# The sign of float64 weights carried by the slope of a parametric ReLU

## The chip, the cores and the metric

The kernel runs on one core of one Trainium2 chip. A core has five engines that run side by side and wait for each other through semaphores: TensorE (PE) for matrix products, VectorE (DVE) and ScalarE (ACT) for element-wise work, GpSimd (POOL) for more element-wise work, and SyncE (SP), which here only issues DMAs. The metric is the time of one execution on the device, in microseconds (us).

## The reference

Chunked attention over 4 x 8 heads of 576 tokens, and then two MLPs on the 2304 tokens, of 512 to 2048 to 512 channels. Cut to what matters:

```python
scores = scale * np.matmul(q_c, k_c.transpose(0, 1, 2, 4, 3))     # chunks of 64 tokens
attn = np.exp(scores - np.max(scores, axis=-1, keepdims=True))
attn = attn / (np.sum(attn, axis=-1, keepdims=True) + 1e-09)
x = np.matmul(attn, v_c)                                          # then tokens x 512

h = x @ w_in                                                      # first MLP
x = (h * (1.0 / (1.0 + np.exp(-1.702 * h)))) @ w_out
h = x @ w_in2                                                     # second MLP: mish
out = (h * np.tanh(np.log1p(np.exp(h)))) @ w_out2
```

q, k and v are float32. The four weight matrices are float64, 8 MB each, since they are drawn as `np.random.randn(...) * c` without a cast.

## The kernel before

**Weights.** No engine computes in float64, so the kernel takes the weights as pairs of 32-bit words and builds float32 from them. Each MLP's weights are 32 pieces of 128 x 512 values (512 KB of float64), which alternate between `w_in` and `w_out`. A piece passes four stages, the methods of class `Weights`:
- `load` (L118, L123): a DMA issued by SP brings the words into a tile `raw`, the low and the high word of each value side by side.
- `scale` (L149): ACT multiplies the high word, read as a float32, by 2^-112. That takes 896 off the eleven-bit exponent. The line is `nc.scalar.mul`, which becomes one ACTIVATE.
- `join` (L159, L160, L163): three DVE instructions. L159 (a TENSOR_SCALAR) shifts the low word right by 29. L160 (a SCALAR_TENSOR_TENSOR) takes the sign bit out of the scaled high word and puts it into the low word. L163 (a SCALAR_TENSOR_TENSOR) shifts the high word left by 3, which pushes its own sign bit out, and puts the low word into it. The result is the float32.
- `split` (L184, L185): the products run as float32r in two parts, so ACT writes the rounded part (L184, a CAST), and POOL writes the rest (L185, a subtraction of two tensors).

For the second MLP the float32 goes back to DRAM between `join` and `split`.

**Stages in time.** Tokens run in 6 blocks of 384. The start, to about 130 us, holds the attention of the first block, the conversion of all 32 pieces of the first MLP, the first MLP's products on block 0 (16 steps of 128 hidden channels), and the attention of block 1. Then the first MLP runs over the other blocks while the pieces of the second are scaled and joined one every two steps. The second MLP fills the rest.

**Order.** Instructions are issued to each engine in the order in which they are written, with no scheduler. The first part of the start is written out in the string `PLAN`, one letter for each call (`c` scale, `j` join, `s` split, `l` load). After it comes a loop over steps; `convert()` is called twice in each of the first 16 steps, and each call splits one piece, joins the next and scales the one after. A step of the first block holds, on PE, 12 products for the in-projection (L337 to L339, tile `h`) and 12 for the out-projection (tile `acc`); on ACT a gelu (L355) and a cast (L359); on POOL the subtraction for the low part of the activations (`g_lo`, L364). Every five steps hold the attention of one tile of 128 tokens: transposes (L246), scores (L262), `shift` (L276, L277), exp (L282), sums, `normalize` on POOL (L293), transposes again, the products with v (L313), and `x_hi`, `x_lo` (L329, L333). ACT's exp and gelu need different tables, so an ACT_TABLE_LOAD stands between them.

Of the kernel before, what the change touches and what calls it, by code (L numbers as in the profile page):

```python
# [11 lines left out]
AF = mybir.ActivationFunctionType  # L12
ALU = mybir.AluOpType
AX = mybir.AxisListType
I32 = mybir.dt.int32
SIGN = -(2**31)

P = 128
CH = 64
TB = 384  # L20
# [4 lines left out]
LAG_B = 5  # L25
GROUP = 4
NRAW = 5
# The start, step by step, where attention, the first products and the weights' conversion share
# the engines: a letter (see `steps`) and the tile, the slot or how often.
PLAN = """  # L30
    w8 d0 d1 w8 T0 T1 w1 Q1 k0 K1 d2 q0 S0 M0 l S1 X0 T2 l v2 M1 N0 K2 l Q2 X1 S2 U0 c N1 c
    M2 j w17 l v0 A0 X2 N2 V0 c c j j v1 l U1 U2 A1 V1 P0 A2 d3 P1 s H0 V2 c w2 H1 s L0 P2 s
# [11 lines left out]
def tile_kernel(  # L44
# [8 lines left out]
    w_out2: bass.AP,  # L53
    out: bass.AP,
):
    """Chunked attention and two MLPs on one stream of tokens, in blocks of TB tokens.

    The products of the MLPs split each float32 operand exactly into two float32r parts and
    carry hi*hi, hi*lo and lo*hi. The first MLP runs over all blocks, with the attention of
    the next block between its products; then its weights give way to the second MLP's.  # L60
    """
    nc = tc.nc
    B, H, S, D = q.shape
    NT, DM = out.shape
# [7 lines left out]
    scale = 1.0 / math.sqrt(D)  # L72
# [9 lines left out]
    ident = const.tile([P, P], F32, name="ident")  # L82
    one = const.tile([P, 1], F32, name="one")

    # ---------------------------------------------------------------- weights
    class Weights:
        """The weights of one MLP, piece by piece: float64 words to float32r hi and lo.

        A float64's high word, read as a float32, has the upper eight bits of the exponent as
        its exponent; 2^-112 there takes 896 off the eleven-bit exponent, so that the word  # L90
        shifted up by three, with its sign and the top of the low word, is the float32.
        """

        def __init__(self, w_in, w_out, staged):
            self.w_in, self.w_out = w_in, w_out
# [31 lines left out]
            self.raw[i] = r  # L127

        def room(self, name):
            """Room for words: at first where the last half of the weights goes later."""  # L130
            if len(self.spare) > self.np // 2:
                return wres.tile([P, DM, 2], I32, tag=self.spare.pop(), name=name)
            return wraw.tile([P, DM, 2], I32, tag="raw", name=name)

        def load_ahead(self):
            """Loads for which there is room by now."""
            used = self.at["join" if self.staged is not None else "split"]
            while self.at["load"] < self.np and (
                len(self.spare) > KF or self.at["load"] - max(used, self.first) < self.ahead
            ):  # L140
                self.load()
                if len(self.spare) > KF:
                    self.first = self.at["load"]

        def scale(self):
            if (i := self._next("scale")) is None:
                return
            hi = self.raw[i][:, :, 1].bitcast(F32)
            nc.scalar.mul(hi, hi, 2.0**-112)  # L149

        def join(self):
            if (i := self._next("join")) is None:
                return
            r = self.raw.pop(i)
            lo, hi = r[:, :, 0], r[:, :, 1]
            to = hi
            if self.staged is not None:
                to = half_slot(f"wf{i}").bitcast(I32)
            nc.vector.tensor_scalar(lo, lo, 29, None, op0=ALU.logical_shift_right)  # L159
            nc.vector.scalar_tensor_tensor(  # L160
                lo, hi, SIGN, lo, op0=ALU.bitwise_and, op1=ALU.bitwise_or
            )
            nc.vector.scalar_tensor_tensor(  # L163
                to, hi, 3, lo, op0=ALU.logical_shift_left, op1=ALU.bitwise_or
            )
            if self.staged is not None:
                nc.sync.dma_start(out=self.staged[i], in_=to.bitcast(F32))
            else:
                self.f32[i] = to.bitcast(F32)
# [7 lines left out]
        def split(self):  # L177
            if (i := self._next("split")) is None:
                return
            key = kind, f = self.order[i]  # L180
            w = self.f32.pop(i)
            both = wres.tile([P, 2, DM], F32R, tag=f"w{kind}{f}", name=f"w{kind}{f}")
            hi, lo = both[:, 0], both[:, 1]
            nc.scalar.copy(hi, w)  # L184
            nc.gpsimd.tensor_tensor(out=lo, in0=w, in1=hi.bitcast(F32), op=ALU.subtract)  # L185
            self.hi[key], self.lo[key] = hi, lo

        def convert(self):
            """One step of the pieces on their way: each stage takes the next piece."""
            if self.at["join"] > self.at["split"] and self.staged is None:  # L190
                self.split()
            if self.at["scale"] > self.at["join"]:
                self.join()
            if self.at["load"] > self.at["scale"]:
                self.scale()
            if self.staged is not None or self.at["load"] > 4:
                self.load_ahead()

    def half_slot(name, t=None):
        t = wraw.tile([P, DM, 2], I32, tag="raw", name=name) if t is None else t  # L200
        return t.rearrange("p f w -> p (f w)")[:, 0:DM].bitcast(F32)

    # ---------------------------------------------------------------- attention
    xh, xl = {}, {}

    def load_tok(pool, tag, src, i):
        """128 tokens of all heads, token by partition."""
        t = pool.tile([P, H * D], F32, tag=tag, name=f"{tag}{i}")
        load_into(t, src, i)
        return t  # L210

    def load_into(t, src, i):
        done = 0
        while done < P:
            b, s = divmod(i * P + done, S)
            n = min(P - done, S - s)
            nc.sync.dma_start(
                out=t[done : done + n].rearrange("p (h d) -> p h d", h=H),
                in_=src[b, :, s : s + n, :].rearrange("h p d -> p h d"),
            )  # L220
            done += n

    class Attention:
        """The attention of 128 tokens, two chunks, for all heads: x^T in two parts."""

        def __init__(self, i, slots):
            self.i, self.slots = i, slots
# [53 lines left out]
        def exp(self):  # L281
            nc.scalar.activation(self.eg, self.eg, AF.Exp, scale=scale)  # L282
# [49 lines left out]
            hi, lo = self.xo  # L332
            nc.vector.tensor_tensor(out=lo, in0=self.x, in1=hi.bitcast(F32), op=ALU.subtract)  # L333

    # ---------------------------------------------------------------- products
    def mm3(o, wh, wl, mh, ml, start, stop):
        nc.tensor.matmul(o, wh, mh, start=start, stop=False)  # L337
        nc.tensor.matmul(o, wh, ml, start=False, stop=False)  # L338
        nc.tensor.matmul(o, wl, mh, start=False, stop=stop)  # L339
# [116 lines left out]
            r0 = j * TB + t * P  # L456
            nc.sync.dma_start(out=out[r0 : r0 + P, :], in_=o)

    # ---------------------------------------------------------------- program
    W = [Weights(w_in1, w_out1, False), Weights(w_in2, w_out2, True)]  # L460
    order_b = list(kept) + list(range(NB - 2))
    NA = NB * KF
# [6 lines left out]
    with tc.manual_schedule():  # L469
        at = at_cm.__enter__()  # L470
        every = ["at", "acc0", "acc1"]
        usual = ["at"]
        first = [Attention(i, every) for i in range(TT)]
# [5 lines left out]
        zeros = const.tile([P, TB], BF16, name="zeros")  # L479
# [3 lines left out]
        idle = ps.tile([P, TB], F32, tag="h", name="idle")  # L483
# [12 lines left out]
            load_into(tiles[i].v, v, i)  # L496

        def keep_warm(n):
            """Products of zeros while the data is on its way: an idle array halves its clock."""
            for _ in range(n):  # L500
                nc.tensor.matmul(idle, zeros[:, 0:P], zeros, start=True, stop=True)

# [3 lines left out]
        def split():  # L506
# [5 lines left out]
        steps = {  # L512
            "w": keep_warm,
            "d": load_tile,
            "v": load_v,
            "l": lambda _: w1.load(),
            "c": lambda _: w1.scale(),
            "j": lambda _: w1.join(),
            "s": lambda _: split(),
            "T": lambda i: tiles[i].transposes(),  # L520
# [31 lines left out]
        ends = set(range(NA + FIRST - 1, N - LAST, GROUP)) | {N - LAST - 1, N - 1}  # L552

        def lag(n):
            """How far the out-projection is behind: more from the last block of the first MLP on."""
            if n < NA - KF + LAG_A:
                return LAG_A
            return LAG_T if n < NA + LAG_T else LAG_B


        for n in range(4, N + LAG_B):
            f = n % KF
            # in-projection and activation
            if n < NA:
                j = n // KF
                hp[n] = in_proj(W[0], (xh[j], xl[j]), f)
# [5 lines left out]
            elif n < N:  # L572
# [6 lines left out]
                if n in ends:  # L579
# [5 lines left out]
                    for m in group:  # L585
                        mish_out(m)
                    group.clear()
            # the attention of the next block
            if n < NA - KF and f > 0:
                at_step = (f - 1) % 5  # L590
                if at_step == 0:
# [15 lines left out]
                elif at_step == 4:  # L607
# [1 line left out]
                    att.x_hi(act)  # L609
                    att.x_lo()  # L610
                    att = nxt
            # out-projection
            m = n - lag(n)
            if 0 <= m < NA and m == done:
                done += 1
# [3 lines left out]
            elif m >= NA:  # L619
# [4 lines left out]
                    out_b([m - 1, m], jb)  # L624
                if m % KF == KF - 1:
                    evac_b(jb)
            # weights that run ahead
            if n < KF:
                W[0].convert()
                if n == KF - 1:  # L630
# [10 lines left out]
            else:  # L641
                for _ in range(2):
# [4 lines left out]
                        break  # L647
                    W[1].split()
                    W[1].fetch()
            # room for the second MLP  # L650
            if n == NA - KF:
                at_cm.__exit__(None, None, None)
                tb = ctx.enter_context(tc.tile_pool(name="tb", bufs=5))
# [34 lines left out]
```

## Time and profile before

| | |
|---|---|
| median of 3 runs | 923.54 us (923.38 to 923.80) |
| the profiled execution: span from first to last instruction | 920.4 us |
| the median above that span | 3.1 us |
| PE busy | 884.2 us, 96% |
| DVE busy | 586.0 us, 64% |
| ACT busy | 435.2 us, 47% |
| POOL busy | 225.3 us, 24% |

No time of the profiled execution beyond its span is given, so the 3.1 us between its span and the median are taken as what lies around it.

The shares are means over a program whose stages differ: of the 40 slices of the page, 23 us each, DVE is at 90% or more in the second to the fifth, and below 80% in all others. In the chain of waits, each piece is the work that released the next one. A row of a timeline gives the start, the duration, the engine, the line, and in brackets the idle time just before and what ended it. Matmuls overlap each other, so their pitch (from start to start) is shorter than their duration.

### The profile page before, as it was taken

The numbers are of one execution on the slowest core, as the hardware profiler recorded it, in microseconds if no ns is written. First come the engines' busy times: TensorE is split into PE (matmuls) and PEld (weight loads), VectorE is DVE, ScalarE is ACT, GpSimd is POOL, SyncE is SP. The second block draws the span as 40 slices with busy tenths as digits, with TensorE's granted clock in tenths as the row PEclk, the third lists the DMA queues.
The fourth block names the chain that finished last, engine by engine and source line by source line (L and its number), as shares of the span: only waits on it lengthen the run. The fifth ranks groups of instructions, "written<-read, shape, count | busy, mean of one in ns | idle before, by whom it ended". The sixth has DMA issues, their size and how long they took to land.

```text
span 920.4 us, 14445 instructions
## 1 busy us (share of the span) xinstructions
PE 884.2 (96%) x5724; PEld 823.3 (89%) x5724; DVE 586.0 (64%) x986; ACT 435.2 (47%) x710; POOL 225.3 (24%) x188
## 2 busy tenths in 40 slices
PE   7768889999999999999999999999999999999997
PEld 5767779999999999999999989898989898989896
DVE  6999955456455655646532676676666766766765
ACT  5566644334333333433334654644645545546453
POOL 2565650000000000000156432231221322312312
PEclk9979899999999999999999999999999999999999
DMA  9926642445444633642344101001001001000000
GB/s 244 271 72 183 178 130 101 107 107 178 129 104 131 178 114 94 194 116 70 115 128 124 35 1 69 36 0 69 35 1 69 35 1 70 35 1 0 35 1 35
DMA packets 91940, 82.73 MB, mean 90 GB/s; under 512 B 58848, under 2 KB 75232, under 8 KB 91872
## 3 DMA queue, kind: packets, MB, share of 16 engines
q1 hardware_dynamic: 91872, 81.80, 30.8%
q8 instruction: 45, 0.74, 0.3%
q14 instruction: 23, 0.19, 0.1%
HBM read 62.39 MB, written 19.40 MB: 89 GB/s over the span
## 4 chain that ended last, share of the span: by engine, by line
PE 81%; DVE 12%; ACT 3%; issue 3%; DMA 1%; SPq 0%; POOLq 0%; DVEq 0%; ACTq 0%
PE h L337 13%; PE h L339 13%; PE h L338 13%; PE acc L337 7%; PE acc L338 6%; PE acc L339 6%; PE accb L447 4%; PE accb L446 4%; PE accb L445 4%; DVE raw L160 3%; DVE raw L163 3%; PE third L446 2%; PE third L447 2%; PE third L445 2%; DVE raw L159 2%
## 5 line engine op out<-in xcount | busy, mean ns | idle before, releaser
L337 PE MATMUL h<-xh,wi 128*128 128x384 f32 x512 | 173.9, 340 | 6.7 <-ACT t L355 5.2
L426 POOL TENSOR_TENSOR gl<-e,gh 128x384 fp32r<-128x384 f32 x96 | 108.4, 1129 | 288.0 <-DVE gh L425 286.6
L339 PE MATMUL h<-xh,wi 128*128 128x384 f32 x512 | 173.5, 339 | 1.0 <-POOL wi L185 1.0
L338 PE MATMUL h<-xl,wi 128*128 128x384 f32 x512 | 172.9, 338 | 0.7 <-DVE xl L333 0.7
L337 PE MATMUL acc<-gh,wo 128*128 128x384 f32 x384 | 135.5, 353 | 0.0
L359 DVE CAST gh<-t 128x384 fp32r<-128x384 f32 x80 | 34.5, 431 | 157.8 <-ACT t L355 156.6
L417 ACT ACTIVATE e<-e,one 128x384 f32<-128x384 f32 x96 | 59.2, 617 | 159.3 <-DVE e L412 159.2
L338 PE MATMUL acc<-gl,wo 128*128 128x384 f32 x384 | 129.7, 338 | 0.0
L339 PE MATMUL acc<-gh,wo 128*128 128x384 f32 x384 | 129.5, 337 | 0.0
L355 ACT ACTIVATE t<-h 128x384 f32<-128x384 f32 x96 | 47.1, 490 | 172.1 <-PE h L339 83.6
L337 PEld LDWEIGHTS h<-xh,wi 128*128 128x128 f32 x512 | 97.3, 190 | 9.9 <-ACT t L355 5.8
L338 PEld LDWEIGHTS h<-xl,wi 128*128 128x128 f32 x512 | 97.2, 190 | 1.9 <-DVE xl L333 1.1
L185 POOL TENSOR_TENSOR wi<-ws,wi 128x512 fp32r<-128x512 f32 x16 | 21.1, 1319 | 316.9 <-ACT wi L184 316.9
L339 PEld LDWEIGHTS h<-xh,wi 128*128 128x128 f32 x512 | 97.2, 190 | 1.4 <-POOL wi L185 1.3
L418 DVE TENSOR_TENSOR e<-e,hs 128x384 f32<-128x384 f32 x96 | 54.2, 564 | 64.1 <-ACT e L417 64.1
L337 PE MATMUL h<-x2h,wi 128*128 128x384 f32 x256 | 86.3, 337 | 0.0
L339 PE MATMUL h<-x2h,wi 128*128 128x384 f32 x256 | 86.2, 337 | 0.0
L338 PE MATMUL h<-x2l,wi 128*128 128x384 f32 x256 | 85.9, 336 | 0.0
L425 DVE CAST gh<-e 128x384 fp32r<-128x384 f32 x96 | 79.6, 829 | 9.4 <-DVE e L424 0.5
L447 PE MATMUL accb<-wo,gl 128*128 128x512 f32 x192 | 76.4, 398 | 1.0 <-POOL gl L426 1.0
L446 PE MATMUL accb<-wo,gh 128*128 128x512 f32 x192 | 75.8, 395 | 0.0
L337 PEld LDWEIGHTS acc<-gh,wo 128*128 128x128 f32 x384 | 73.1, 190 | 2.0
(97 smaller groups left out, 1668.5 us busy)
## 6 DMA issues: line engine op xcount, KB each, us to landing
raw<-in_moe_w_in_dram SPq DMA_DIRECT2D x32, 512.0 KB, 4.0
raw<-in_moe_w_out_dram SPq DMA_DIRECT2D x32, 512.0 KB, 3.8
w_f<-wf SPq DMA_DIRECT2D x32, 256.0 KB, 2.2
ws<-w_f SPq DMA_DIRECT2D x32, 256.0 KB, 2.7
out_dram<-o SPq DMA_DIRECT2D x18, 256.0 KB, 2.1
v<-in_v_dram SPq DMA_DIRECT2D x16, 256.0 KB, 5.7
q<-in_q_dram SPq DMA_DIRECT2D x13, 256.0 KB, 4.7
k<-in_k_dram SPq DMA_DIRECT2D x13, 256.0 KB, 5.3
```

Of the source, the lines that this page charges most:

```text
L337: nc.tensor.matmul(o, wh, mh, start=start, stop=False)
L338: nc.tensor.matmul(o, wh, ml, start=False, stop=False)
L339: nc.tensor.matmul(o, wl, mh, start=False, stop=stop)
L355: nc.scalar.activation(gt[n], hp.pop(n), AF.Gelu_apprx_sigmoid)
L359: (nc.scalar.copy if n < KF else nc.vector.tensor_copy)(gh[n], gt[n])
L417: nc.scalar.activation(e, e, AF.Ln, bias=one, scale=0.5)
L418: nc.vector.tensor_add(e, e, hs[n])
L425: nc.vector.tensor_copy(out=a, in_=z)
L426: nc.gpsimd.tensor_tensor(out=b, in0=z, in1=a.bitcast(F32), op=ALU.subtract)
L445: nc.tensor.matmul(o, a[:, ts], wh, start=f == 0, stop=False)
L446: nc.tensor.matmul(o, a[:, ts], wl, start=False, stop=False)
L447: nc.tensor.matmul(o, b[:, ts], wh, start=False, stop=f == KF - 1)
```

## The change

The scaling step becomes a parametric ReLU with scale 2^-112 and slope 2^32. A positive word is scaled as before. A negative word is scaled by 2^-112 and then by 2^32, which adds 32 to its eight-bit exponent; that sets bit 28 of the word, and the shift left by 3 in `join` moves bit 28 to bit 31, the sign of the float32. So L160 is no longer issued, 32 times for each MLP, 64 in all. Comments and docstrings are dropped as well; lines behind `join` have numbers lower by three in the changed kernel, where L160 is the step that is L163 before.

```diff
-SIGN = -(2**31)
...
             hi = self.raw[i][:, :, 1].bitcast(F32)
-            nc.scalar.mul(hi, hi, 2.0**-112)
+            nc.scalar.activation(hi, hi, AF.Prelu, scale=2.0**-112, alpha=2.0**32)
...
             nc.vector.tensor_scalar(lo, lo, 29, None, op0=ALU.logical_shift_right)
             nc.vector.scalar_tensor_tensor(
-                lo, hi, SIGN, lo, op0=ALU.bitwise_and, op1=ALU.bitwise_or
-            )
-            nc.vector.scalar_tensor_tensor(
                 to, hi, 3, lo, op0=ALU.logical_shift_left, op1=ALU.bitwise_or
             )
```

On DVE, in the loop of the first 16 steps, before the change (the number behind a tile's name counts tiles; three pieces and the `x_lo` of one attention tile):

```order
L159 TENSOR_SCALAR raw_588<-raw_588 128x512
L160 SCALAR_TENSOR_TENSOR raw_588<-raw_588 128x512
L163 SCALAR_TENSOR_TENSOR raw_588<-raw_588 128x512
L333 TENSOR_TENSOR xl_723<-pv_705,xh_722 128x2x4x64
L159 TENSOR_SCALAR raw_599<-raw_599 128x512
L160 SCALAR_TENSOR_TENSOR raw_599<-raw_599 128x512
L163 SCALAR_TENSOR_TENSOR raw_599<-raw_599 128x512
L159 TENSOR_SCALAR raw_641<-raw_641 128x512
L160 SCALAR_TENSOR_TENSOR raw_641<-raw_641 128x512
L163 SCALAR_TENSOR_TENSOR raw_641<-raw_641 128x512
```

The same place after it:

```order
L159 TENSOR_SCALAR raw_578<-raw_578 128x512
L160 SCALAR_TENSOR_TENSOR raw_578<-raw_578 128x512
L330 TENSOR_TENSOR xl_708<-pv_690,xh_707 128x2x4x64
L159 TENSOR_SCALAR raw_588<-raw_588 128x512
L160 SCALAR_TENSOR_TENSOR raw_588<-raw_588 128x512
L159 TENSOR_SCALAR raw_628<-raw_628 128x512
L160 SCALAR_TENSOR_TENSOR raw_628<-raw_628 128x512
```

One of three instructions of each piece is gone; nothing else on DVE stands in another place. On ACT, around the first exp among the gelus, before the change:

```order
L149 ACTIVATE raw_363<-raw_363 128x512
L282 ACT_TABLE_LOAD
L282 ACTIVATE e_502<-e_502 128x512
L184 CAST wo_581<-raw_359 128x512
L184 CAST wi_585<-raw_361 128x512
L355 ACT_TABLE_LOAD
L355 ACTIVATE t_593<-h_539 128x384
L149 ACTIVATE raw_365<-raw_365 128x512
```

And after it:

```order
L149 ACTIVATE raw_360<-raw_360 128x512
L279 ACT_TABLE_LOAD
L279 ACTIVATE e_496<-e_496 128x512
L181 CAST wo_571<-raw_356 128x512
L181 CAST wi_575<-raw_358 128x512
L352 ACT_TABLE_LOAD
L352 ACTIVATE t_582<-h_531 128x384
L149 ACTIVATE raw_362<-raw_362 128x512
```

No table load is added, there or anywhere else on ACT, and none moves. The orders of PE, POOL and SP are the same before and after.

## Rows read from the trace of the kernel before

**Rows 1.** The page: busy tenths of DVE in 40 slices of 23 us.
```profile
DVE  6999955456455655646532676676666766766765
```
**Rows 2.** Stretches: busy us (count) of PE, PEld, DVE, ACT, POOL; clock; DMA share, GB/s.
```profile
16.00:128.00 112.00, 84.74 (x655) 77.86 (x653) 105.78 (x120) 69.27 (x116) 68.26 (x50) 0.90 0.64 180
62.33:97.51 35.18, 26.89 (x200) 24.97 (x199) 33.13 (x37) 21.88 (x37) 22.94 (x16) 0.95 0.59 169
140.00:300.00 160.00, 160.00 (x1287) 155.42 (x1286) 89.43 (x169) 60.88 (x94) 0.00 (x0) 1.00 0.46 125
50.00:55.00 5.00, 2.06 (x8) 2.06 (x9) 4.79 (x7) 3.01 (x4) 2.77 (x2) 0.50 0.00 0
```
**Rows 3.** The chain of waits in order of time: start us, us, what.
```profile
59.27 1.62 DVE raw L160
...
130.28 0.69 PE pv L313 x32
...
144.54 1.08 PE sc L262 x32
...
168.80 1.08 PE sc L262 x32
```
**Rows 4.** Groups by line, DVE, 16 to 128 us: busy us, mean ns, idle before.
```profile
L163 DVE SCALAR_TENSOR_TENSOR raw<-raw 128x512 int32<-128x512 int32 x32 | 45.4, 1419 | 1.1
L160 DVE SCALAR_TENSOR_TENSOR raw<-raw 128x512 int32<-128x512 int32 x32 | 33.2, 1038 | 3.2 <-ACT wo L184 0.5
L159 DVE TENSOR_SCALAR raw<-raw 128x512 int32<-128x512 int32 x32 | 18.7, 586 | 0.0
```
**Rows 5.** Timeline of DVE: start us, us, engine, line, operation.
```profile
62.21 0.42 DVE L159 TENSOR_SCALAR raw<-raw 128x512 int32<-128x512 int32 x1
62.73 0.69 DVE L160 SCALAR_TENSOR_TENSOR raw<-raw 128x512 int32<-128x512 int32 x1
63.46 1.69 DVE L163 SCALAR_TENSOR_TENSOR raw<-raw 128x512 int32<-128x512 int32 x1
65.07 0.41 DVE L159 TENSOR_SCALAR raw<-raw 128x512 int32<-128x512 int32 x1
...
97.40 0.42 DVE L159 TENSOR_SCALAR raw<-raw 128x512 int32<-128x512 int32 x1
```
**Rows 6.** Timeline of POOL, two places.
```profile
63.06 1.54 POOL L185 TENSOR_TENSOR wo<-raw,wo 128x512 fp32r<-128x512 f32 x1 [1.33 <-ACT wo L184]
...
91.31 1.06 POOL L364 TENSOR_TENSOR gl<-t,gh 128x384 fp32r<-128x384 f32 x1 [1.50 <-ACT gh L359]
92.33 1.75 POOL L185 TENSOR_TENSOR wo<-raw,wo 128x512 fp32r<-128x512 f32 x1
```
**Rows 7.** Timeline of SP, PE and ACT: loads, and what uses them.
```profile
20.17 0.37 SPq L217 DMA_DIRECT2D k<-in_k_dram  x1
...
27.08 1.11 PE L246 MATMUL tr<-ident,q 128*128 128x128 f32 x4
...
87.01 0.37 SPq L118 DMA_DIRECT2D raw<-in_moe_w_in_dram  x1
...
93.52 0.70 ACT L149 ACTIVATE raw<-raw 128x512 f32<-128x512 f32 x1
```
**Rows 8.** The page: DMA issues, KB each, median us to landing.
```profile
raw<-in_moe_w_in_dram SPq DMA_DIRECT2D x32, 512.0 KB, 4.0
...
k<-in_k_dram SPq DMA_DIRECT2D x13, 256.0 KB, 5.3
```
**Rows 9.** Groups by line, ACT, whole run.
```profile
L149 ACT ACTIVATE raw<-raw 128x512 f32<-128x512 f32 x64 | 43.0, 675 | 0.0
L282 ACT ACT_TABLE_LOAD x15 | 19.2, 1283 | 0.2
L282 ACT ACTIVATE e<-e 128x512 f32<-128x512 f32 x17 | 10.8, 633 | 15.7 <-DVE e L277 15.7
```
**Rows 10.** Groups by line, DVE, 142 to 466 us.
```profile
L160 DVE SCALAR_TENSOR_TENSOR raw<-raw 128x512 int32<-128x512 int32 x32 | 22.2, 694 | 1.2
```

## Prediction

> **What bounds the kernel now.** I read the page first. DVE's row of busy tenths [rows 1] has two parts: 9 in the second to the fifth slice, 23 to 115 us, and 3 to 7 in all behind. So I cut the run near there. In the stretches [rows 2] DVE is busy for 105.8 of the 112.0 us from 16 to 128, PE for only 84.7 and ACT for 69.3; from 140 to 300 it is PE that has no idle time at all, 160.00 of 160.00. The start is DVE's, the rest is PE's. The chain of waits, read third, says the same in order of time: up to 128 us it consists of DVE's joins, such as L160 at 59.27, and from 130.28 on of PE [rows 3].
>
> The groups by line [rows 4] then tell what DVE does there: of its 105.8 us, 97.3 are the three instructions of the 32 joins (45.4 + 33.2 + 18.7). A piece in the loop starts at 62.21 and the next at 65.07, 2.86 us later [rows 5]. The stretch repeats itself every five steps, ten pieces and one attention tile: from 62.21 to 97.40, 35.19 us [rows 5]. PE does five such steps in 24.26 us where nothing holds it up (scores to scores, 144.54 to 168.80 [rows 3]), and ACT is busy for 21.9 us of such a cycle [rows 2]. So in the start DVE has 11 us a cycle to lose before PE is next.
>
> **What is removed.** L160, 64 times. The first 32 lie in the DVE stretch. Alone it takes 0.69 us, and the next instruction starts 0.73 us behind its start (62.73 to 63.46 [rows 5]). Its mean is 1038 ns though, and L163's 1419 [rows 4], with 1.69 in the row at 63.46 [rows 5]. The extra microsecond is POOL's: its subtraction L185 starts at 63.06, while L160 runs [rows 6], and L163 behind it is stretched by 1.00 us. Two POOL instructions back to back start 1.02 us apart (91.31 and 92.33 [rows 6]), so that is how long one holds DVE up. The Trainium skill has this as a rule (SBUF — State Buffer, section "Who interferes with whom"): a VectorE instruction with two inputs in SBUF and a GpSimd instruction that reads SBUF exclude each other for a whole instruction, and whichever starts first goes first. The trace agrees, with the 1.00 us above. By the rule POOL's holds outlive the instruction that they fell on, and the gain is 23.4 us; by L160's own recorded time it would be 34.
>
> The sum over the three lines: stretched time is 33.2 - 32 x 0.69 = 11.1 us in L160, 45.4 - 32 x 0.69 = 23.3 in L163, 18.7 - 32 x 0.42 = 5.3 in L159, together 39.7 us. POOL has some 50 instructions in the stretch [rows 2], at 1.02 us 51 us; the rest of these falls beside DVE work that it does not disturb. POOL's work isn't touched by the change, so I let its 39.7 us stand, on L163 and L159 instead of L160, and count only the unstretched pitch: 32 x 0.73 = 23.4 us. The other end is that L160's stretched time goes too: 33.2 + 32 x 0.03 between instructions = 34.2 us. I take 23.4, because the same POOL instructions have to fit into a shorter time.
>
> The wait of 0.10 us that L160 has behind L159 (3.2 us of idle time in 32 [rows 4]) isn't gained: L163 now follows L159 and waits in its place. It also takes over L160's wait for ACT's scaling, behind the same DVE instructions as before; nothing new is queued behind it.
>
> The 32 joins of the second MLP lie at 142 to 466 us [rows 10]. DVE is at 89 of 160 us there and PE at 160 [rows 2]; PE's products hide them, and I count nothing. Without that cover it would be another 23.4 us.
>
> **What is late next.** Two terms go off the 23.4.
> - The transposes of the fourth attention tile ran at 27.08, and its k was issued at 20.17 [rows 7]; with the 5.3 us to landing [rows 8] it is there at 25.5, so the transposes can come 1.6 us earlier. Three joins ahead of them give 2.2. I take off 0.6.
> - DVE has 112.0 - 105.8 = 6.2 us of idle time in the stretch, at the exps and casts that it waits for. With the cycle at 35.19 - 7.3 = 27.9 us, ACT goes from 62% to 78% of it, so these waits grow. I take a third more, 2.1 us, an estimate; its ends are nothing and a doubling, 6.2.
>
> Weight loads stay hidden: a load issued at 87.01 is used by ACT at 93.52 [rows 7], 6.5 us later, and lands after 4.0 [rows 8]. Shrunk as the cycle does (27.9 / 35.19) the 6.5 are 5.2, still enough. If such loads came late by 1 us a cycle, it would cost some 3 us in all.
>
> **What is added.** A slope, on ACT, in the same 64 instructions. No row shows a parametric ReLU. The nearest are the scaling itself, 675 ns on the same tile, and the exp on as many elements, 633; on the other side an instruction of 675 with a table load of 1283 in front of each, 1958 ns [rows 9]. I take 675: the tile is the same and exp, a real curve, isn't dearer. ACT has 35.18 - 21.88 = 13.3 us of idle time a cycle [rows 2], so a few hundredths more or less are hidden.
>
> **Sum.** 23.4 - 0.6 - 2.1 = 20.7 us off the span of 920.4, that is 899.7. The median of the runs is 3.1 us above that span, and I keep that: 902.8 us.
>
> **Rivals.**
> - More gain. L160's stretched part goes as well, 34.2 us, since POOL's holds fall beside the attention's DVE work or the waits. For it: in the stretch some 11 us of POOL's 51 are harmless already. It ends at PE: the cycle would be 35.19 - 10 x 1.07 = 24.5 us, and PE needs 24.26. With the two terms off, 34.2 - 2.7 = 31.5, 892.0 us.
> - Less gain: PE's clock takes over the bound. From 50 to 55 us PE is granted 0.50 of its speed, 1.2 instead of 2.4 GHz, after it has been waiting; over the cycle it has 0.95 [rows 2]. Below 24.26 / 27.9 = 0.87 PE is slower than DVE. At 0.75, a cycle takes 32.3 us and gains 2.9; there are (128 - 62) / 35.19 = 1.9 of them, 5.4 us, and the 13 joins before 62 us give 9.5 - 0.6. Together 14.3, 909.2 us. Against it: a shorter DVE cycle leaves PE fewer and shorter waits, and those come before each fall.
> - Slower: the parametric ReLU is dear on ACT. It decides from 13.3 / 10 = 1.33 us a piece, where ACT has no idle time left. With a table load for each piece (1.28 us [rows 9]; a gelu stands between every two pairs) a cycle has 21.9 + 12.8 = 34.7 us of ACT work. If half of the 13.3 us of waits stays, that is 41.4 and 6.2 more than now, 11.6 over 1.9 cycles, 935 us. Against it: the order on ACT has the same loads in the same places. The Trainium skill (ScalarE: Activation LUTs, section "What ACT_TABLE_LOAD costs") puts a switch at 2.66 us with the drain behind it, twice the 1283 ns of the trace; by that figure this rival is dearer still.
>
> Were the slope not applied at all, the same instructions would run, and the time would be as forecast.
>
> **How the numbers follow.** Forecast 72%, with 898 to 908 us as its own range, from the bounds of the two terms and of a few microseconds of POOL's holds. More gain 11%, less gain 11%, dear ReLU 6%. To leave out no more than 2 in 10, the range goes most of the way to the two neighbours: 893 to 910. About 0.2%, 1.8 us, is what a measurement of this kernel can tell from no change. The first three cases are all faster, 94%; of the last, 4% is slower and 2% ends within 0.2%.
>
> **What would show it.** Right: the last join of the first MLP ends at some 107 us instead of 128; the cycle in the loop is 28 to 29 us; the second instruction of a join has a mean well over 1 us, as much as L163 has now or more, as POOL's holds move to it; ACT's scaling stays at 0.65 to 0.70 us; the pitch of PE behind the start is the same 24.26 us. Wrong: the scaling takes over 1 us, or a table load stands before it; the cycle is below 26 us (POOL's holds went too) or above 31, with PE's clock below 0.87 in it; DVE's idle time in front of a join ends with a DMA.

## The result and the profile after

The changed kernel takes 898.41 us (897.90 to 899.08, 4 runs), beside 923.46 us of the kernel before in the same comparison: a ratio of 0.9731, 95% interval 0.9718 to 0.9744. That is 25.0 us less where 20.7 were forecast; the forecast time was 902.8 us, and the range 893 to 910. The profiled execution has a span of 896.3 us, 24.1 less than before.

The page's row of DVE's busy tenths, in slices that are now 22.4 us long, as in [rows 1]:

```profile
DVE  5989654454455455445333766766767767757755
```

The second to the fourth slice have 9, 8 and 9, and the fifth 6; before, all four had 9. The stretches that answer to [rows 2], with the same columns (busy us of PE, PEld, DVE, ACT, POOL, then the clock and the DMAs): the one that DVE bounds, from the first join to the last, one cycle of five steps in it, and the two that were shown of before:

```profile
16.29:104.22 87.93, 75.00 (x654) 70.29 (x652) 81.18 (x88) 68.30 (x116) 66.97 (x48) 1.00 0.79 222
57.43:85.46 28.03, 24.68 (x196) 23.45 (x196) 26.33 (x28) 21.29 (x37) 22.64 (x17) 1.00 0.74 209
140.00:300.00 160.00, 160.00 (x1288) 155.42 (x1287) 78.74 (x155) 59.77 (x93) 0.00 (x0) 1.00 0.48 133
50.00:55.00 5.00, 3.89 (x51) 3.82 (x52) 4.79 (x5) 3.16 (x7) 3.67 (x4) 1.00 0.57 180
```

The stretch is 87.9 us long instead of 112.0, which is as much as the span lost, 24.1 us. DVE's busy time in it went from 105.8 to 81.2, 24.6 less, and its idle time from 6.2 to 6.8. The cycle takes 28.03 us instead of 35.19. Behind the stretch PE has no idle time, as before. From 50 to 55 us PE was granted half its clock before (0.50, 1.2 GHz); now it is granted all of it (1.00, 2.4 GHz), as over the whole stretch. DVE's timeline at the 14th join, around that cycle, and at the end of the last join (columns as in [rows 5]; L160 is now the step that was L163):

```profile
51.15 1.23 DVE L159 TENSOR_SCALAR raw<-raw 128x512 int32<-128x512 int32 x1
...
57.43 0.42 DVE L159 TENSOR_SCALAR raw<-raw 128x512 int32<-128x512 int32 x1
57.88 1.68 DVE L160 SCALAR_TENSOR_TENSOR raw<-raw 128x512 int32<-128x512 int32 x1
59.48 0.42 DVE L159 TENSOR_SCALAR raw<-raw 128x512 int32<-128x512 int32 x1
60.00 0.69 DVE L160 SCALAR_TENSOR_TENSOR raw<-raw 128x512 int32<-128x512 int32 x1
60.61 1.55 DVE L159 TENSOR_SCALAR raw<-raw 128x512 int32<-128x512 int32 x1
62.26 1.32 DVE L160 SCALAR_TENSOR_TENSOR raw<-raw 128x512 int32<-128x512 int32 x1
...
85.46 0.64 DVE L159 TENSOR_SCALAR raw<-raw 128x512 int32<-128x512 int32 x1
...
103.53 0.69 DVE L160 SCALAR_TENSOR_TENSOR raw<-raw 128x512 int32<-128x512 int32 x1
```

The chain of waits passes from DVE to PE at 106 us where it did so at 130 [rows 3], and the pitch of PE from scores to scores behind that is the same, 24.25 us:

```profile
103.54 0.69 DVE raw L160
...
106.39 0.69 PE pv L310 x32
...
120.66 1.08 PE sc L259 x32
...
144.91 1.08 PE sc L259 x32
```

The pitch was 24.26 us before. In the timeline the stretched rows are still there, with about the same microsecond on top, but on other instructions: L159, which was 0.42 us in most joins before, is now about 1.55 in a third of them. The groups by line of DVE in the stretch show it in sum, beside [rows 4]:

```profile
L160 DVE SCALAR_TENSOR_TENSOR raw<-raw 128x512 int32<-128x512 int32 x32 | 42.1, 1315 | 3.2 <-ACT raw L149 0.5
L159 DVE TENSOR_SCALAR raw<-raw 128x512 int32<-128x512 int32 x32 | 30.5, 952 | 0.0
```

Stretched time is 42.1 - 32 x 0.69 = 20.0 us and 30.5 - 32 x 0.42 = 17.1, together 37.1, where the three lines had 39.7. And the idle 3.2 us in front of the last step are the same, now in front of the other instruction. ACT's scaling over the whole run, beside [rows 9]:

```profile
L149 ACT ACTIVATE raw<-raw 128x512 f32<-128x512 f32 x64 | 43.1, 677 | 0.3
L279 ACT ACT_TABLE_LOAD x15 | 19.2, 1283 | 0.3
```

That is 677 ns instead of 675, and 15 table loads at the exps as before.

### The profile page after: what moved, and what is told of

The parts are those of the page before. It is cut to its first block, busy times and chain, and to the rows that moved or that the text cites. A ratio compares the mean times of both kernels' runs of the same rounds, so it can differ in the third digit from the quotient of the medians.

```text
span 896.3 us, 14381 instructions
## 1 busy us (share of the span) xinstructions
PE 874.3 (98%) x5724; PEld 815.5 (91%) x5724; DVE 538.6 (60%) x922; ACT 434.1 (48%) x710; POOL 224.7 (25%) x188
## 4 chain that ended last, share of the span: by engine, by line
PE 84%; DVE 9%; ACT 3%; issue 2%; POOLq 0%; DVEq 0%; ACTq 0%
PE h L334 13%; PE h L336 13%; PE h L335 13%; PE acc L334 7%; PE acc L335 6%; PE acc L336 6%; PE accb L444 5%; PE accb L443 4%; PE accb L442 4%; DVE raw L160 2%; PE third L443 2%; PE third L444 2%; PE third L442 2%; DVE raw L159 2%; PE sc L259 2%
## 5 line engine op out<-in xcount | busy, mean ns | idle before, releaser
L334 PE MATMUL h<-xh,wi 128*128 128x384 f32 x512 | 171.9, 336 | 0.9 <-DVE hs L408 0.9
L336 PE MATMUL h<-xh,wi 128*128 128x384 f32 x512 | 171.6, 335 | 0.0
L334 PEld LDWEIGHTS h<-xh,wi 128*128 128x128 f32 x512 | 96.1, 188 | 3.5 <-DVE hs L408 2.2
L336 PEld LDWEIGHTS h<-xh,wi 128*128 128x128 f32 x512 | 96.1, 188 | 0.0
L443 PE MATMUL accb<-wo,gh 128*128 128x512 f32 x192 | 75.8, 395 | 0.0
L442 PE MATMUL accb<-wo,gh 128*128 128x512 f32 x192 | 74.7, 389 | 0.1
```

The costliest lines, as they stand in the source:

```text
L442: nc.tensor.matmul(o, a[:, ts], wh, start=f == 0, stop=False)
L443: nc.tensor.matmul(o, a[:, ts], wl, start=False, stop=False)
```

## The experiments

Theory 1 is the forecast's: in the stretch that DVE bounds, each sign step costs its unstretched pitch of 0.73 us, POOL's holds stay and only move, the slope costs nothing, and the 32 steps of the second MLP are hidden. Its rivals are named in each expectation. All times stand beside the kernel before on the same chip, at 922.5 to 923.8 us.

**Which half of the steps.** The change for one MLP's weights alone:

```diff
# first only: in scale() and join()
+if self.staged is None:
     nc.scalar.activation(hi, hi, AF.Prelu, scale=2.0**-112, alpha=2.0**32)
+else:
+    nc.scalar.mul(hi, hi, 2.0**-112)
...
+if self.staged is not None:
     nc.vector.scalar_tensor_tensor(lo, hi, SIGN, lo, op0=ALU.bitwise_and, op1=ALU.bitwise_or)
# second only: the two conditions exchanged
```

> The change for the first MLP's weights alone; the second MLP's keep the multiplication and the sign step. Theory 1, the gain is the unstretched pitch of 32 sign steps in the stretch that DVE bounds (32 x 0.73 us), and the other 32 are hidden behind PE: 898.4 us, all of the gain. Rival, the gain comes from less DVE and POOL load over the whole of the first MLP, in proportion to the steps removed: about 911.

> The change for the second MLP's weights alone. Theory 1: 923.5 us, as before, since PE has no idle time where these 32 steps lie. Rival, gain in proportion: about 911.

The first alone took 898.61 us, ratio 0.9744 (0.9727 to 0.9761); the second alone 923.29, ratio 1.0003 (0.9993 to 1.0012). The whole gain is in the first MLP's 32 steps, and the 22.2 us of busy time that left DVE behind the stretch [rows 10] were worth nothing.

**The price of the slope.** The ReLU with the sign step kept, and the multiplication with the sign step left out:

```diff
# prelu and sign: the kernel before, with
-nc.scalar.mul(hi, hi, 2.0**-112)
+nc.scalar.activation(hi, hi, AF.Prelu, scale=2.0**-112, alpha=2.0**32)
# mul and no sign: the changed kernel, with the line of before
```

> The parametric ReLU in the scaling step, and DVE's sign step kept, 64 times each; the result is the same. Theory 1, the slope costs nothing on ACT: 923.5 us, with the scaling at 0.68 us in the stretch. Rival, the ReLU is dearer than the multiplication and ate part of the gain: above 925, with a scaling above 0.75 us.

> The sign step left out and the plain multiplication kept: the weights lose their signs, so this leaves out part of the computation. Theory 1: 898.4 us, as with the ReLU. Rival, the ReLU ate part of the gain: below 896.

They took 923.02 us, ratio 0.9999 (0.9990 to 1.0008), and 898.20 us, ratio 0.9734 (0.9720 to 0.9749). ACT's scaling in the first of them, from 16 to 129 us:

```profile
L149 ACT ACTIVATE raw<-raw 128x512 f32<-128x512 f32 x30 | 20.5, 685 | 0.0
```

It is 685 ns in the second too. So the slope is free to within the 0.1% that the intervals leave, from both sides: added without the removal it changes nothing, and taken away with the removal it gives nothing.

**The price of a step, from the other side.** The kernel before with the sign step issued twice in the first MLP:

```diff
 nc.vector.scalar_tensor_tensor(lo, hi, SIGN, lo, op0=ALU.bitwise_and, op1=ALU.bitwise_or)
+if self.staged is None:
+    nc.vector.scalar_tensor_tensor(lo, hi, SIGN, lo, op0=ALU.bitwise_and, op1=ALU.bitwise_or)
```

> The kernel before, with the sign step issued twice for each piece of the first MLP; the result is the same. Theory 1, such a step costs its unstretched pitch of 0.73 us and POOL's holds only move: 32 x 0.73 = 23.4 more, 946.9 us. Rival, it costs its whole recorded time with POOL's holds (1.04 + 0.03 us): 34.2 more, 957.7 us.

It took 950.21 us, ratio 1.0290 (1.0275 to 1.0305): 26.4 more, far from the rival's 34.2 and 3.0 above theory 1. DVE's groups from 16 to 158 us; L164 is the second sign step and L167 the last step:

```profile
L164 DVE SCALAR_TENSOR_TENSOR raw<-raw 128x512 int32<-128x512 int32 x32 | 48.5, 1516 | 1.1
L160 DVE SCALAR_TENSOR_TENSOR raw<-raw 128x512 int32<-128x512 int32 x32 | 31.0, 969 | 2.8
L167 DVE SCALAR_TENSOR_TENSOR raw<-raw 128x512 int32<-128x512 int32 x32 | 29.0, 907 | 1.1
L159 DVE TENSOR_SCALAR raw<-raw 128x512 int32<-128x512 int32 x32 | 14.0, 437 | 0.0
```

The stretched time is 26.4 + 8.9 + 6.9 + 0.6 = 42.8 us here, 39.7 with one sign step, 37.1 with none. So POOL's holds do move, but not quite as a whole: about 3 us of them come and go with 32 steps. 23.4 + 3.1 = 26.5 is the measured 26.4. I think that with more DVE work in a join fewer of POOL's instructions fall beside DVE work that they do not disturb; that wasn't tried apart.

**Whether the stretch is POOL's.** In the changed kernel, POOL's reading taken away:

```diff
-nc.gpsimd.tensor_tensor(out=lo, in0=w, in1=hi.bitcast(F32), op=ALU.subtract)
+nc.gpsimd.memset(lo.bitcast(F32), 0.0)      # first MLP only
```

> The changed kernel, and POOL's subtraction for the low part of the first MLP's weights (32 instructions that read two tensors in SBUF) replaced by a memset of zeros; this leaves out the low parts. Theory 1, the stretched time of DVE's joins (37.1 us in the changed kernel) is POOL's reading: the cycle of five steps falls from 28.0 us to PE's 24.3 to 25, 3.1 cycles of it, so about 888 us, and the joins' means fall to about 0.45 and 0.8 us. Rival, the stretch is DVE's own or another engine's: 898.4.

It took 888.85 us, ratio 0.9628 (0.9612 to 0.9644), as theory 1 has it. A cycle takes 24.94 us, the first row; the second and third are DVE's groups from 16 to 93 us, where the joins end:

```profile
52.04:76.98 24.94, 23.76 (x193) 23.02 (x194) 15.43 (x28) 21.32 (x38) 10.93 (x18) 1.00 0.79 225
```
```profile
L160 DVE SCALAR_TENSOR_TENSOR raw<-raw 128x512 int32<-128x512 int32 x32 | 26.0, 811 | 10.8 <-ACT raw L149 8.3 <-ACT wo L181 0.5
L159 DVE TENSOR_SCALAR raw<-raw 128x512 int32<-128x512 int32 x32 | 21.6, 675 | 0.5 <-DMA raw<-in_moe_w_in_dram 0.5
```

The stretched time falls from 37.1 us to 3.9 + 8.2 = 12.1, and DVE no longer bounds the cycle: it is busy for 15.4 of 24.9 us, PE for 23.8, and DVE now waits for ACT's scaling (8.3 us from 16 to 93 us). The last step's mean fell to 811 ns as expected; L159's fell only to 675 and not to 450. So 25.0 of the 37.1 us, two thirds of the stretched time, went with the reading of these 32 instructions; POOL's other subtractions and multiplications are still there, and L159's part is told of under the surprises.

**Whether DVE still bounds after the change.** In the changed kernel, each shift one join earlier:

```diff
 def join(self):
+    self.shift_low(i)                      # unless it has been issued
+    if self.staged is None and i + 1 in self.raw:
+        self.shift_low(i + 1)              # L159 of the next piece
     ...
-    nc.vector.tensor_scalar(lo, lo, 29, None, op0=ALU.logical_shift_right)
```

> The changed kernel, and each shift of a low word issued one join earlier, ahead of the previous piece's last step, so that the 0.10 us that a step waits for the shift in front of it is filled. Theory 1, DVE still bounds the stretch: 32 x 0.10 = 3.2 us less, 895.2 us. Rival, after the change PE, ACT or the weight loads bound it already: 898.4 us.

It took 897.23 us, ratio 0.9725 (0.9706 to 0.9744): 1.2 us less than the change, with intervals that overlap, so neither the 3.2 nor the rival is shown. (That DVE still bounds is more plainly seen from the run before: 9.6 us went with most of POOL's holds.) The waits of DVE from 16 to 105 us (who waited for whom: us in total, times, longest) tell where part of it went:

```profile
DVE raw L155 <- DMA raw<-in_moe_w_in_dram: 4.4, 5, 1.8
...
DVE raw L155 <- DMA raw<-in_moe_w_out_dram: 1.8, 4, 0.5
```

The groups by line over the same time, where L169 is the last step and L155 the shift:

```profile
L169 DVE SCALAR_TENSOR_TENSOR raw<-raw 128x512 int32<-128x512 int32 x32 | 43.3, 1355 | 0.2 <-ACT raw L150 0.2
L155 DVE TENSOR_SCALAR raw<-raw 128x512 int32<-128x512 int32 x32 | 25.7, 805 | 6.2 <-DMA raw<-in_moe_w_in_dram 4.4 <-DMA raw<-in_moe_w_out_dram 1.8
```

The idle time in front of the last step went from 3.2 to 0.2 us, but the shift, a join ahead, meets weight loads that have not landed, for 6.2 us. The loads were early enough for the order that was, and not for this one. That the version isn't slower goes with the stretched time, which is 21.2 + 12.3 = 33.5 us instead of 37.1; why it is less wasn't tried apart.

**POOL's work on DVE.** If a hold costs DVE more than the work itself, DVE can do it. The low parts of the first MLP's weights go to DVE, each one join later (`low on DVE`); the low parts of the first block's activations too (`all on DVE`, with the shift ahead, and `no ahead` without it); or the activations' alone:

```diff
 # split(): weights
-nc.gpsimd.tensor_tensor(out=lo, in0=w, in1=hi.bitcast(F32), op=ALU.subtract)
+self.late.append((lo, w, hi))      # first MLP; nc.vector does it behind the next join
 # g_lo(): activations
-eng = nc.gpsimd if n < KF else nc.vector
+eng = nc.vector
```

> The changed kernel with the shift one join ahead, and with the low parts of the first MLP's weights and of the first block's activations subtracted on DVE (0.61 us pitch each, the weights' one join later) instead of on POOL. Theory 1, a POOL instruction costs DVE about 0.76 us of stretch here, more than the same work on DVE: the cycle of five steps falls from 28.0 us to about 24.5, near PE's 24.26, so about 889 us. Rival, DVE's own work counts in full and POOL's was beside it: 32 x 0.61 + 16 x 0.5 more and 3.2 less, 923 us.

> The changed kernel with the low parts of the first MLP's weights and of the first block's activations on DVE as in the run before, but each shift in its own join again. Theory 1, there the shifts a join ahead waited for weight loads (3.9 us of idle time ended by DMAs), which gave back what they saved: about 892 us, no slower than 893.1. Rival, the shift ahead was worth its 3.2 us there too: 896.

> The changed kernel with the low parts of the first MLP's weights alone on DVE, the activations' on POOL as before. Theory 1, 32 POOL holds of about 0.76 us go and 32 instructions of 0.61 us pitch come: 3 to 5 us less than the change, 894 us. Rival, DVE's own work counts in full: 918 us.

> The changed kernel with the low parts of the first block's activations alone on DVE, the weights' on POOL as before. Theory 1, 16 POOL holds of 0.76 us go and 16 instructions of 0.5 us come, but DVE now waits in its order for gelu and the cast on ACT: between 894 and 898.4. Rival, DVE's own work counts in full: 906 us.

All on DVE: 893.14 us, ratio 0.9672 (0.9658 to 0.9687), 4 us short of the expectation; DVE waits there 4.3 us for ACT's cast of the activations and 3.8 us for weight loads. Without the shift ahead: 895.20, ratio 0.9704 (0.9691 to 0.9717), a miss: I expected the shift ahead to be worth nothing there, and it was worth 2.1 us by the times and 3.0 by the ratios (the two ran on different chips), near the rival's 3.2. The weights' alone: 891.92, ratio 0.9664 (0.9651 to 0.9677), 2 us better than expected. The activations' alone: 901.70, ratio 0.9774 (0.9760 to 0.9787), slower than the change by 3.3 us and a miss again, between the expectation and its rival's 906. Its waits of DVE from 16 to 105 us:

```profile
DVE gl L361 <- ACT gh L356: 9.2, 9, 2.2
DVE sm L284 <- ACT e L279: 1.4, 2, 0.7
```

The activations' subtraction needs ACT's cast, which is late; on POOL that wait held up nothing, on DVE the next join stands behind it, for 9.2 us (6.5 in `no ahead`). To move the activations' subtraction as well costs 3.3 us on top of the change, and 3.3 on top of `low on DVE` (895.20 against 891.92). So the weights' alone measures the hold best, though DVE waits for ACT's casts there too (4.3 us, third row). DVE's groups there, from 16 to 107 us (L172 is the subtraction, L161 the last step):

```profile
L161 DVE SCALAR_TENSOR_TENSOR raw<-raw 128x512 int32<-128x512 int32 x32 | 28.6, 895 | 2.6
L160 DVE TENSOR_SCALAR raw<-raw 128x512 int32<-128x512 int32 x32 | 14.6, 457 | 0.0
L172 DVE TENSOR_TENSOR wo<-raw,wo 128x512 fp32r<-128x512 f32 x16 | 11.7, 737 | 4.3 <-ACT wo L188 4.3
L172 DVE TENSOR_TENSOR wi<-raw,wi 128x512 fp32r<-128x512 f32 x16 | 11.7, 736 | 0.0
```

Stretched time is 6.5 + 1.2 + 1.3 = 9.0 us instead of 37.1: by this difference 32 POOL instructions had cost DVE 28.1 us, 0.88 each, and the same work on DVE costs about 0.6 us as a pitch and 0.69 as a duration, unstretched.

**The fastest version.** The weights' low parts on DVE, and the shift one join ahead:

> The fastest version so far (the weights' low parts on DVE, the activations' on POOL) with each shift one join ahead. Theory 1 with what the earlier runs showed: the 0.10 us in front of each join's last step are filled, 2.6 us of idle time in that version, and part of it comes back as waits of the early shifts for weight loads, 2 to 4 us in the runs that had them: 890 to 892 us. Rival, the loads are late by more than the shift saves: 893 or above.

It took 890.46 us, ratio 0.9654 (0.9641 to 0.9667), as expected: 8.0 us below the change and 32.0 below the kernel before on its chip. Against `low on DVE` it is 1.5 us, with intervals that overlap, so what the shift ahead gives here isn't shown.

## Why the prediction was right

- **The total.** 898.41 us lies 4.4 us below the forecast of 902.8 and 6.4 above the rival "more gain", 892.0, so the time alone hardly tells the two apart. The rows do: of 39.7 us of stretched time 37.1 were left.
- **The bound.** Right: the 24.1 us of the span are the 24.1 us by which DVE's stretch got shorter, and only the first MLP's steps count (898.61 alone, against 923.29).
- **The price of a step, 23.4 us for 32.** Right as a pitch. The rival "more gain", by which all 11.1 us of L160's stretched time go, fell: doubling the step cost 26.4 us and not 34.2.
- **"I let its 39.7 us stand."** The term that was mis-sized most: 37.1 us of POOL's holds stayed, 2.6 went. They also went elsewhere than was said. The second instruction of a join was to have a mean as large as L163's 1419 ns or larger; it has 1315, and the shift's went from 586 to 952. The excess of the gain lies ahead of the loop's cycles: a cycle lost 7.2 us where ten steps make 7.3, but the 14th join starts at 51.15 us instead of 62.21, 11.1 earlier, where 13 steps make 9.5. Of the 2.6 us of holds some 2 went there; why wasn't tried.
- **The waits that grow, 2.1 us.** The size is near, the reading was wrong. The 6.2 us of idle time were not all waits for exps and casts: 1.4 us were for exps and 0.5 for a cast, and most of the rest were the short gaps between dependent instructions, 3.2 us in front of L160 (that cast's 0.5 among them) and 1.1 in front of L163. DVE's idle time went from 6.2 to 6.8 us, though the 1.1 us (part of the 23.4) had gone from it, so waits grew by 1.7. The waits for exps stayed at 1.4, and one of 0.5 for ACT stayed. What is new is one wait, for `x_hi` of an attention tile:

```profile
54.13 0.67 ACT L181 CAST wi<-raw 128x512 fp32r<-128x512 f32 x1 [1.61 <-DVE raw L160]
56.21 0.58 ACT L326 CAST xh<-pv 128x512 fp32r<-128x512 f32 x1
56.82 0.69 DVE L330 TENSOR_TENSOR xl<-pv,xh 128x512 fp32r<-128x512 f32 x1 [1.58 <-ACT xh L326]
```

ACT's cast waits for the end of a join; scaling, gelu, the gelu's cast and `x_hi` follow it without a pause, 2.7 us in all, and DVE has only one join left to do meanwhile. Before the change a join took 2.86 us and covered them; here that join met no hold and took 1.2.

- **The fourth tile's k, 0.6 us.** Misread: the row at 27.08 us is of q's transposes. Those of k were the next, and could come 2.5 us earlier before they met the load, more than the 2.2 that three joins give, so there was nothing to take off. Before the change and after it:

```profile
27.98 1.06 PE L246 MATMUL tr<-ident,k 128*128 128x128 f32 x4
```
```profile
24.66 0.66 PE L243 MATMUL tr<-ident,k 128*128 128x128 f32 x4 [0.26 <-DMA k<-in_k_dram]
```

They came 3.3 us earlier and PE waited 0.3 us for k. DVE lost nothing by it: its first wait for another engine in the stretch is at 47 us.

- **The slope.** Right: 677 ns, and the time doesn't change with it or without it. The rival of the dear ReLU fell.
- **PE's clock.** The rival of less gain fell: the clock in the cycle went up from 0.95 to 1.00, with PE idle for 3.4 us of it instead of 8.3.
- **The weight loads.** Right for this change, with no DMA among DVE's waits; the shift ahead shows how little was left.
- **The sum.** 20.7 us forecast, 2.6 more of the holds and 1.0 more of the waits (1.7 instead of 2.7) are 24.3, beside the 24.1 by which the stretch got shorter; the last join ends at 104.2 us where some 107 were forecast. The 3.1 us around the span were too many as well. In every execution whose span is recorded the time is 1.7 to 1.9 us above it, and executions of the kernel before, which took 921.91 to 924.00 us, have 922.2 where the span is 920.4. So the profiled one was a short one, and some 1.3 us of the 3.1 were the difference between executions; that closes the gap to the 25.0 us of the medians to some tenths.

## What to carry to other kernels

Where one engine bounds a stretch, an instruction taken out of it is worth its pitch without the waits that another engine's work puts on it: those waits move to the next instructions in order (37.1 of 39.7 us here). To be rid of them the other engine's instruction had to go, or to stop reading; here each of POOL's cost DVE 0.88 us, and DVE did the same work in about 0.65, so the faster split had less parallel work in it. But move only work whose inputs are early: in an engine's fixed order a late input holds up all that stands behind.

## What the runs showed of the hardware that I had not expected

POOL's memsets, which read no tensor, still hold up DVE's shift, though not the step that takes two tensors. POOL's and DVE's timelines in the version with memsets, at two places:

```profile
45.68 1.02 POOL L364 TENSOR_TENSOR gl<-t,gh 128x384 fp32r<-128x384 f32 x1 [0.92 <-ACT gh L359]
46.65 0.52 POOL L183 MEMSET wo<- 128x512 f32 x1
47.11 0.52 POOL L183 MEMSET wi<- 128x512 f32 x1
...
63.76 1.05 POOL L293 TENSOR_TENSOR e<-e,rc 128x512 f32<-128x512 f32 x1 [2.25 <-ACT raw L149]
64.74 0.53 POOL L183 MEMSET wo<- 128x512 f32 x1
65.20 0.53 POOL L183 MEMSET wi<- 128x512 f32 x1
```
```profile
45.76 2.15 DVE L159 TENSOR_SCALAR raw<-raw 128x512 int32<-128x512 int32 x1
...
63.87 1.48 DVE L160 SCALAR_TENSOR_TENSOR raw<-raw 128x512 int32<-128x512 int32 x1
65.27 0.74 DVE L159 TENSOR_SCALAR raw<-raw 128x512 int32<-128x512 int32 x1
```

The shift at 45.76 lasts 2.15 us, until POOL's subtraction and both memsets behind it are over, although 0.42 would do. The two-tensor step at 63.87 is held by POOL's multiplication up to some 64.8, but it ends at 65.35, inside the memsets that follow, so those did not hold it. The shift at 65.27 meets the second of them alone, and takes 0.74 us. Of the shift's 17.1 us of stretched time 8.2 stayed in that version, where the last step's went from 20.0 to 3.9. The Trainium skill (SBUF — State Buffer, section "Who interferes with whom") says that an instruction with two inputs in SBUF contends with a GpSimd instruction that reads there, not with one that only writes; the trace agrees in the step at 63.87. By the same section of the Trainium skill a VectorE instruction in a mode that takes both of its ports contends with GpSimd. The shift behaves like one, with 0.74 and 2.15 us beside a memset; in which mode it runs no row shows.
